# A kernel of attention and two expert layers: one weight loaded by 128 rows, one operand in two transfers, exponentials in another order, and a new order of all steps

## The chip, the cores and the metric

The kernel runs on one core of a Trainium2 chip. The metric is the device time of one launch in microseconds (us), the median of several runs. The core has TensorE (PE, whose weight loads are listed as PEld), VectorE (DVE), ScalarE (ACT), GpSimd (POOL) and SyncE (SP), which issues nearly all transfers here, and 16 DMA engines that carry them out.

## What is computed

Attention over a packed set of 32 rows a head, then a gated layer with a rational function, then one with a cosine. The weights and their inputs `w_in`, `w_out` come as float64.

```python
q, k, v: (8, 8, 576, 64)   p: (8, 8, 32, 64)          # batch, heads, sequence, head size
def sm_attn(qq, kk, vv):
    a = softmax(scale * qq @ kk.T)                    # exp(s - max) / (sum + 1e-9)
    return a @ vv
packed = sm_attn(p, k, v)
x = sm_attn(q, packed, packed)                        # -> x: (4608, 512), heads side by side
h = x @ moe_w_in                                      # 512 x 2048
g = (a0 + a1 h + a2 h^2 + a3 h^3) / (1 + |b0||h| + |b1| h^2 + 1e-6)
y = g @ moe_w_out                                     # 2048 x 512
h = y @ moe2_w_in;  out = (h cos h) @ moe2_w_out
```

## The kernel before

**Stages.** Attention works in 16 units, each of one batch entry and four heads. For a unit, SP loads p, k, q and v (`load`, L461 to L477); PE turns k and q (`trans`, L493) and ACT copies them out of PSUM (`copied`); PE makes the scores of p and k (`scores`, L522), DVE takes their maximum, ACT the exponentials and their sum (`exp1`, L540); PE turns the exponentials in five pieces (`turn_exp`, L558 and L560) and multiplies them with v (`pack`, L573). The packed rows, turned, are kept in DRAM (`keep_pack`, L591) and take part in a second set of scores with q, whose normalized form goes to DRAM as well (`keep_attn`, L631).

**Layer 0** doesn't form x. `m_prod` (L719) multiplies a unit's packed rows with the rows of `w_in` that belong to its heads, and `front` (L769) multiplies the attention weights with the result. 128 steps of ACT, DVE and POOL make the rational function, and `back` (L806) multiplies with `w_out`. Layer 1 loads the result again as x and runs `front` (L785) and `back` for nine blocks of 512 tokens. All large products are made from a high and a low part, so that each is three products.

**The float64 weights.** A tile of 128 x 512 numbers comes as raw words into one of two buffers (`w_load`, L372 for layer 0's w_in, L376 for layer 1's, L381 for w_out). `convert` makes float32 of it in five or six steps: ACT `w_exp` (L389) and `w_low` (L392), DVE `w_abs` (L398) and `w_join` (L408), then for most tiles ACT `w_hi` (L415) and POOL `w_lo` (L420). For layer 0's w_in a tile is made of 64 rows of one head for one block of 512 columns on partitions 0 to 63, and the same rows for the next block on partitions 64 to 127: two transfers of 256 KB. The 16 tiles of w_in and of w_out come in an early and a late half each.

**v.** A unit's v has, in each partition, rows that fit the order in which `exp1` leaves its columns: six transfers, four of 32 partitions with four rows each (L471) and two of 32 partitions with one row (L473).

**The order.** Nothing is scheduled by hand. `Plan.add` records each step with its engine, its costs (busy time, a tail, time on a common DMA bus) and a key, the sum of `FIRST` of its group, `EACH` by its number and `WANTED` of its kind. `Plan.order` then plays the program: of each engine's ready steps it takes, among those that can start within 60 ns, the one with the lowest key. The program is issued in the order of the starts, and every engine keeps to it; waits are semaphores. An SP step counts as 60 ns a transfer (300 for v), whatever is in flight. Group "u" are the first two units, "v" the others, "wi" and "wo" the weights of layer 0, "i" layer 0's steps, "j" layer 1's, "k" the conversion of layer 1's w_in.

Of the kernel before, what the change touches and what calls it, by code (L numbers as in the profile page):

```python
# [9 lines left out]
F32 = mybir.dt.float32  # L10
# [18 lines left out]
class Plan:  # L29
# [11 lines left out]
    WINDOW = 60  # L41

    WANTED = {
        "a2_hi": -80, "a2_lo": 439, "a2_load": -168, "absolute": 238, "back 0": -2,
        "back 0 late": -55, "back 1": 104, "clipped": -277, "copied k": -11, "copied q": -9,
        "cosine": -104, "cubic 0": 1422, "cubic 1": -100, "denom": 166, "done1": -495,
        "done2": -76, "doubled": 32, "exp1": 107, "exp2": 350, "exp_copied": -161, "front 0": -355,
        "front 1": -301, "inverse": 10, "keep_attn": -68, "keep_out": -236, "keep_pack": 207,
        "less_max2": -2, "lin 0": -333, "lin 1": -85, "load k": -12, "load p": -45, "load q": 135,
        "load v": -106, "log": 60, "lower 0": -152, "lower 1": 259, "m_hi": 30, "m_lo": 276,  # L50
        "m_load": 169, "m_prod": -278, "max1": -204, "max2": -287, "open_both": -90,
        "open_left": -65, "open_right": -252, "over 0": 953, "over 1": -66, "pack": 412,
        "packed": -67, "ratio": 60, "recip1": -88, "recip2": -264, "reduced 0": 543,
        "reduced 1": 83, "rounded": -18, "scaled2": -323, "scores 0": -198, "scores 1": -25,
        "slope": -6, "store": 170, "sum2": -36, "taken p": -42, "taken pp": 69, "times": -16,
        "trans k": 107, "trans q": 373, "turn2": 5, "turn_back": -126, "turn_exp": 382,
# [25 lines left out]
    def add(self, eng, busy, key, fn, *args, tail=0, r=(), w=(), new=(), after=(), bus=0, late="", opens=()):  # L82
# [3 lines left out]
        key = self.FIRST[group] + self.EACH[group] * i + off + self.WANTED.get(s.kind, 0)  # L86
        s.eng, s.busy, s.ns, s.key, s.fn, s.args, s.bus = eng, busy, busy + tail, key, fn, args, bus
# [42 lines left out]
    def order(self):  # L130
# [7 lines left out]
        bus = 3000  # L138
# [22 lines left out]
        while len(done) < len(self.steps):  # L161
# [15 lines left out]
            if s.bus:  # L177
# [4 lines left out]
            if s.eng != "-":  # L182
# [33 lines left out]
def pack_attention_moe_moe_kernel(  # L216
# [213 lines left out]
    last_conv = [()]  # L430

    def convert(l, f, which, key, after=()):
        x = (l, f, which)
        group, n, off = key
        bus = 2270 if x[::2] == (1, "i") else 2160 if which == "i" else 1270
        add("SP", 120 if x[::2] == (0, "i") else 60, (group, n, off - 4), w_load, *x, new=[("raw", ("raw", *x), [P, 2 * DM], U32)], bus=bus, after=after)
        add("ACT", 560, key, w_exp, *x, tail=100, r=[("raw", *x)], new=[("sc", ("g", *x), [P, DM], F32)], after=last_conv[0])
        add("ACT", 570, key, w_low, *x, tail=100, r=[("raw", *x)], new=[("sc", ("w", *x), *SC)], after=last_conv[0] if x[::2] == (1, "i") or x == (1, 0, "o") else ())
        s = add("DVE", 603, key, w_abs, *x, tail=85, r=[("g", *x)], w=[("w", *x)])
        if (l, which) == (0, "i"):  # L440
            k2, o = divmod(f, 2)
            home = dict(w=[("win1", k2)]) if o else dict(new=[(f"s{k2}", ("win1", k2), [P, 2 * DM], F32)])
            add("DVE", 604, key, w_join, *x, tail=85, r=[("raw", *x), ("w", *x)], **home)
# [16 lines left out]
    def load(u, nm):  # L460
# [5 lines left out]
        elif nm == "v":  # L466
# [3 lines left out]
            for j in range(4):  # L470
                nc.sync.dma_start(t[32 * j : 32 * (j + 1), :, 0:4, :], rows[:, :, 4 * j : 4 * j + 4, :])  # L471
# [58 lines left out]
    def halves(t):  # L530
        return t[:, :, 0:HS]
# [660 lines left out]
```

## Time and profile before

| | us |
|---|---|
| median of 3 runs (1642.66 to 1646.63) | 1646.03 |
| the profiled execution | 1648.32 |
| its span in the trace | 1646.5 |
| PE busy | 1564.8 |
| DVE busy | 1289.8 |
| ACT busy | 1036.8 |

The profile shows one execution. "Busy" is time in which an engine works; a wait is put down to whom it ended with. DMA shares are the time of packets on the 16 DMA engines, and since packets overlap they can pass 1. The clock is the share of PE's full clock that was granted. Attention takes about the first 200 us, layer 0 goes on beside it and then alone to about 870, layer 1 to the end.

### The profile page before, as it was taken

What the parts mean: (1) busy time and instruction counts of PE and PEld (TensorE: products, weight loads), DVE (VectorE), ACT (ScalarE), POOL (GpSimd) and SP (SyncE); (2) the same over time, 40 slices, a digit from 0 to 9 for tenths busy, and PEclk for the clock granted to TensorE, in tenths of its full rate; (3) what the DMA queues carried; (4) which work ended last, traced back from release to release, by engine and by line L of the source; (5) the groups of instructions that cost most, each with busy time, mean ns of one, the idle gap of its engine ahead of it and who ended that gap; (6) DMA issues with size and microseconds to landing.
All of it is one profiled execution on the core that took longest, in us unless ns stands there. A gap on an engine that the chain in (4) does not pass through costs nothing.

```text
span 1646.5 us, 26978 instructions
## 1 busy us (share of the span) xinstructions
PE 1564.8 (95%) x10176; PEld 1340.0 (81%) x10176; DVE 1289.8 (78%) x2025; ACT 1036.8 (63%) x1745; POOL 343.1 (21%) x274
## 2 busy tenths in 40 slices
PE   4677899999999999999999999999999999999998
PEld 3455688899999989998987878888888888888887
DVE  3588999899999999999899876666666667676664
ACT  4588898999999988998866533333333334343332
POOL 1154334334343343333322200000000000000000
PEclk9899999999999999999999999999999999999999
DMA  9899732212223121215344320201010101001010
GB/s 233 225 273 275 200 92 66 71 48 84 87 66 100 41 88 54 75 41 180 107 152 141 86 65 13 56 17 46 17 39 7 45 1 39 13 22 31 1 26 26
DMA packets 100130, 133.63 MB, mean 81 GB/s; under 512 B 22176, under 2 KB 76960, under 8 KB 100000
## 3 DMA queue, kind: packets, MB, share of 16 engines
q1 hardware_dynamic: 99616, 131.38, 27.8%
q8 instruction: 80, 1.31, 0.3%
q10 hardware_dynamic: 384, 0.52, 0.1%
q14 instruction: 50, 0.41, 0.1%
HBM read 94.11 MB, written 37.75 MB: 80 GB/s over the span
## 4 chain that ended last, share of the span: by engine, by line
PE 77%; ACT 8%; DVE 7%; DMA 5%; issue 2%; SPq 1%; POOL 0%; DVEq 0%; ACTq 0%; POOLq 0%
PE acc L806 41%; PE b L785 23%; PE b L769 9%; DMA raw<-in_moe_w_in_dram 2%; PE b L719 2%; DVE T L893 1%; DMA raw<-in_moe_w_out_dram 1%; ACT T L884 1%; DMA v_in<-in_v_dram 1%; DVE T L895 1%; DVE U L918 1%; PE b L493 1%; DVE T L922 1%; DVE T L918 1%; ACT V L898 1%
## 5 line engine op out<-in xcount | busy, mean ns | idle before, releaser
L806 PE MATMUL acc<-gh,wo 128*128 128x288 f32 x2048 | 417.9, 298 | 2.4 <-ACT gh L950 1.9
L806 PE MATMUL acc<-wo,gh 128*128 128x512 f32 x1152 | 354.9, 389 | 1.4 <-POOL wo L420 1.4
L806 PEld LDWEIGHTS acc<-gh,wo 128*128 128x128 f32 x2048 | 328.2, 188 | 25.5 <-issue 16.6
L806 PE MATMUL acc<-gl,wo 128*128 128x288 f32 x1024 | 301.9, 295 | 2.6 <-DVE gl L953 2.6
L907 POOL TENSOR_TENSOR U<-U,V 128x576 f32<-128x576 f32 x128 | 182.5, 1435 | 369.3 <-DVE T L922 107.7
L806 PEld LDWEIGHTS acc<-wo,gh 128*128 128x128 f32 x1152 | 216.2, 188 | 46.5 <-POOL wo L420 1.7
L886 ACT ACTIVATE T<-b 128x512 f32<-128x512 f32 x144 | 86.0, 597 | 256.6 <-PE b L785 256.2
L806 PE MATMUL acc<-wo,gl 128*128 128x512 f32 x576 | 224.2, 389 | 0.0
L926 DVE TENSOR_SCALAR T<-T 128x512 f32<-128x512 f32 x144 | 62.3, 433 | 189.7 <-ACT T L886 189.0
L806 PEld LDWEIGHTS acc<-gl,wo 128*128 128x128 f32 x1024 | 193.1, 189 | 3.8 <-DVE gl L953 3.8
L950 ACT CAST gh<-V 128x512 fp32r<-128x512 f32 x144 | 89.5, 622 | 111.5 <-PE acc L806 107.4
L941 ACT ACTIVATE U<-U 128x512 f32<-128x512 f32 x144 | 90.6, 629 | 80.3 <-DVE U L937 80.1
L806 PEld LDWEIGHTS acc<-wo,gl 128*128 128x128 f32 x576 | 108.2, 188 | 22.4
L944 DVE TENSOR_TENSOR V<-U,b 128x512 f32<-128x512 f32 x144 | 98.6, 684 | 29.5 <-ACT U L941 25.1
L884 ACT ACTIVATE T<-b,par 128x576 f32<-128x576 f32 x128 | 106.3, 830 | 16.8 <-PE b L769 14.8
L953 DVE TENSOR_TENSOR gl<-T,gh 128x576 fp32r<-128x576 f32 x128 | 108.8, 853 | 9.1 <-PE acc L806 4.5
L901 ACT ACTIVATE U<-V,par 128x576 f32<-128x576 f32 x128 | 111.0, 871 | 0.9 <-DVE T L922 0.2
L953 DVE TENSOR_TENSOR gl<-V,gh 128x512 fp32r<-128x512 f32 x144 | 101.0, 702 | 11.6 <-PE acc L806 11.2
L933 DVE SCALAR_TENSOR_TENSOR U<-T,U 128x512 f32<-128x512 f32 x144 | 105.4, 732 | 3.4
L895 DVE SCALAR_TENSOR_TENSOR T<-T,par,b 128x576 f32<-128x576 f32 x128 | 101.0, 808 | 7.8 <-ACT V L898 6.5
L918 DVE SCALAR_TENSOR_TENSOR U<-U,V 128x576 f32<-128x576 f32 x128 | 100.6, 794 | 7.1 <-ACT V L914 6.6
L893 DVE TENSOR_TENSOR T<-T,b 128x576 f32<-128x576 f32 x128 | 92.9, 745 | 15.8 <-ACT T L884 8.2
(182 smaller groups left out, 3092.8 us busy)
## 6 DMA issues: line engine op xcount, KB each, us to landing
raw<-in_moe_w_out_dram SPq DMA_DIRECT2D x32, 512.0 KB, 3.8
x<-ob SPq DMA_DIRECT2D x24, 576.0 KB, 3.5
k_in<-in_k_dram SPq DMA_DIRECT2D x16, 576.0 KB, 5.7
q_in<-in_q_dram SPq DMA_DIRECT2D x16, 576.0 KB, 7.6
raw<-in_moe_w_in_dram SPq DMA_DIRECT2D x32, 256.0 KB, 5.4
v_in<-in_v_dram SPq DMA_DIRECT2D x64, 128.0 KB, 6.1
raw<-in_moe_w_in_dram SPq DMA_DIRECT2D x16, 512.0 KB, 4.7
w<-sc SPq DMA_DIRECT2D x32, 256.0 KB, 2.2
```

The lines of the kernel that those rows point to most:

```text
L769: nc.tensor.matmul(TILE["h", j][:, e, 0:HS], lhsT=w[:, o : o + P], rhs=x[:, g, :], start=n == 0, stop=n == 3 * NG - 1,)
L785: nc.tensor.matmul(h, lhsT=w[:, ks], rhs=x, start=n == 0, stop=n == 3 * KC - 1)
L806: nc.tensor.matmul(o, lhsT=w, rhs=x, start=i == first and n == 0, stop=i == last and n == len(todo) - 1,)
L884: nc.scalar.activation(T, hidden(j), AF.Identity, scale=par[:, 3:4], bias=par[:, 2:3])
L893: nc.vector.tensor_tensor(T, T, h, op=ALU.mult)
L895: nc.vector.scalar_tensor_tensor(T, T, par[:, 1:2], h, op0=ALU.add, op1=ALU.mult)
L901: nc.scalar.activation(shaped(j, "U"), shaped(j, "V"), AF.Identity, scale=par[:, 5:6], bias=par[:, 4:5])
L907: return nc.gpsimd.tensor_tensor(Q, Q, V, op=ALU.mult)
L918: return nc.vector.scalar_tensor_tensor(t, t, add_, shaped(j, "V"), op0=ALU.add, op1=ALU.mult)
L933: return nc.vector.scalar_tensor_tensor(Y, T, -C2, Y, op0=ALU.mult, op1=ALU.add)
L944: nc.vector.tensor_tensor(shaped(j, "V"), shaped(j, "U"), hidden(j), op=ALU.mult)
L953: return nc.vector.tensor_tensor(shaped(j, "gl"), result(j), shaped(j, "gh").bitcast(F32), op=ALU.subtract)
```

## The change

- **w_in (layer 0):** a tile is now 128 successive rows, those of two heads, for one block of 512 columns, in one transfer of 512 KB onto 128 partitions. Tile t holds heads 2t and 2t+1 for the even block and 2t+1 and 2t+2 for the odd one; where the rows pass 512 (2 of 16 tiles) two transfers remain. `m_prod` finds a head's rows with `rows_at`, so its row halves alternate from product to product, and it reads three tiles where it read two.
- **v:** two transfers a unit: rows 4r to 4r+3 onto partition r for all 128 partitions (512 KB, 1 KB runs), and the last 64 rows onto 64 partitions.
- **Exponentials:** `exp1` writes its results in the order of the keys (a step of 18 elements within a row), so that `turn_exp` reads every fourth element for its four pieces; its last piece is one transpose of 64 columns in place of two products of 32. The pieces of k are no longer turned in a special order.
- **Order:** the planner holds SP to eight transfers in flight and counts 480 ns an issue (`RING`, `ISSUE`), several costs and DMA times are other numbers, the loads of weights are kept in sequence, more kinds of step have a key of their own ("late", "E"), and a table `SHIFT` adds to the key by unit or item. All keys are new.

```diff
+    RING, ISSUE = 8, 480
     WANTED = {
...
     FIRST = {
-        "i": 702.05, "j": 1208.14, "k": 2019.64, "u": -2236.31, "v": -638.77, "wi": -8864.36,
-        "wi late": -3070.04, "wo": -3690.94, "wo late": 1155.49,
+        "i": 220.69, "j": 453.76, "k": 1649.06, "u": -144.84, "v": 113.95, "wi": -3610.16,
+        "wi late": -1623.51, "wo": 597.92, "wo late": -1411.71,
     }
...
+        if group in self.SHIFT:
+            key += self.SHIFT[group][max(0, int(i) // self.PER.get(group, 1))]
...
+            if s.eng == "SP":
+                t = max(t, landed[-self.RING])
...
+            if s.eng == "SP":
+                n, at = s.busy // self.ISSUE, a
+                for _ in range(n):
+                    at = max(at, landed[-self.RING])
+                    bus = max(bus, at + 600) + s.bus / n
+                    landed.append(bus + 1400)
+                    at += self.ISSUE
+                s.end, free["SP"] = bus + 1400, at
...
-            a, h = divmod(f, H)
-            for e in range(2):
-                n = 2 * a + e
-                nc.sync.dma_start(
-                    r64[e * D : (e + 1) * D, :], w_in1[h * D : (h + 1) * D, n * DM : (n + 1) * DM]
-                )
+            t, e = divmod(f, 2)
+            a, t = divmod(t, KC)
+            cols = slice((2 * a + e) * DM, (2 * a + e + 1) * DM)
+            rows = (2 * t + e) * D
+            if rows + P <= DM:
+                nc.sync.dma_start(r64, w_in1[rows : rows + P, cols])
+            else:
+                nc.sync.dma_start(r64[0:D], w_in1[rows : rows + D, cols])
+                nc.sync.dma_start(r64[D:P], w_in1[0:D, cols])
...
-            rows = v[b, hs].rearrange("h (p c) d -> p h c d", c=2 * NT9)
-            for j in range(4):
-                nc.sync.dma_start(t[32 * j : 32 * (j + 1), :, 0:4, :], rows[:, :, 4 * j : 4 * j + 4, :])
-            for e in range(2):
-                nc.sync.dma_start(t[32 * e : 32 * (e + 1), :, 4, :], rows[:, :, 16 + e, :])
+            main = 4 * P
+            nc.sync.dma_start(
+                t[:, :, 0:4, :].rearrange("r h c d -> r h (c d)"),
+                v[b, hs][:, 0:main, :].rearrange("h (r c) d -> r h (c d)", c=4),
+            )
+            nc.sync.dma_start(t[0:D, :, 4, :], v[b, hs][:, main:S, :].rearrange("h r d -> r h d"))
...
-            TILE["e1", u].rearrange("p (a b) -> p a b", a=2),
-            halves(TILE["s", u, 0]),
+            TILE["e1", u].rearrange("r (p t e) -> r e t p", t=NT9, e=2),
+            halves(TILE["s", u, 0]).rearrange("r e (t p) -> r e t p", t=NT9),
...
-        for c in range(4 if a == 0 else 2):
-            first = c % 2 * HS + (c // 2 * P if a == 0 else 2 * P)
-            if a == 0:
-                nc.tensor.transpose(ps[:, c * P : (c + 1) * P], e1[:, first : first + P], ident)
-            else:
-                nc.tensor.matmul(ps[32 * c : 32 * (c + 1), 0:P], lhsT=e1[:, first : first + 32], rhs=ident, start=True, stop=True)
+        if a == 0:
+            for c in range(4):
+                nc.tensor.transpose(ps[:, c * P : (c + 1) * P], e1[:, c : c + 4 * (P - 1) + 1 : 4], ident)
+        else:
+            nc.tensor.transpose(ps[0:D, 0:P], e1[:, 4 * P : S], ident)
...
+    def rows_at(g, h, e):
+        t, half = divmod((g * G4 + h - e) % H, 2)
+        return t, slice(half * D, (half + 1) * D)
...
-                k2, o = divmod(a * H + g * G4 + h, 2)
+                t, rows = rows_at(g, h, e)
...
-                    rhs=TILE["win1", k2][rows, o * DM : (o + 1) * DM],
+                    rhs=TILE["win1", a * KC + t][rows, e * DM : (e + 1) * DM],
```

## Rows read from the trace of the kernel before

**Rows 1.** The page: busy us (share), then tenths of 40 slices of the span.

```profile
PE 1564.8 (95%) x10176; PEld 1340.0 (81%) x10176; DVE 1289.8 (78%) x2025; ACT 1036.8 (63%) x1745; POOL 343.1 (21%) x274
...
DMA  9899732212223121215344320201010101001010
```

**Rows 2.** Engines by stretch: from:to, length, busy PE, PEld, DVE, ACT, POOL, clock, DMA share, GB/s.

```profile
10.00:80.00 70.00, 46.61 (x644) 29.10 (x645) 35.31 (x73) 37.88 (x76) 11.02 (x16) 0.90 0.92 238
80.00:190.00 110.00, 91.57 (x1215) 65.59 (x1212) 94.96 (x175) 93.78 (x180) 54.31 (x50) 0.95 0.92 257
190.00:220.00 30.00, 20.86 (x124) 18.68 (x117) 28.08 (x43) 25.27 (x43) 8.23 (x6) 0.89 0.60 167
220.00:400.00 180.00, 173.57 (x1329) 163.79 (x1329) 164.28 (x223) 164.71 (x272) 68.47 (x49) 0.99 0.20 64
400.00:760.00 360.00, 358.11 (x2818) 339.33 (x2817) 339.54 (x462) 330.98 (x529) 129.12 (x92) 1.00 0.25 80
760.00:880.00 120.00, 112.48 (x740) 103.85 (x739) 107.54 (x156) 94.07 (x155) 40.30 (x30) 1.00 0.42 131
```

**Rows 3.** The chain of waits from 10 to 80 us, shares by line.

```profile
by line: DMA raw<-in_moe_w_in_dram 31.5%; DMA k_in<-in_k_dram 14.8%; PE b L493 13.2%; DMA v_in<-in_v_dram 9.0%; PE b L522 6.8%; PE one L573 5.1%; ACT qT L499 3.0%; ACT kT L499 2.8%; PE b L719 2.8%; ACT sc L392 2.6%; ACT sc L389 2.2%; PE one
```

**Rows 4.** As rows 2, one transfer alone: v; k and q; w_in; layer 1's w_in.

```profile
8.00:10.00 2.00, 0.00 (x0) 0.00 (x0) 1.27 (x2) 0.97 (x3) 0.00 (x0) 1.00 1.07 211
...
16.00:20.00 4.00, 2.71 (x13) 2.07 (x12) 0.00 (x0) 1.37 (x4) 0.00 (x0) 1.00 1.02 417
...
22.00:25.00 3.00, 2.31 (x31) 1.27 (x24) 1.11 (x4) 1.32 (x3) 0.00 (x0) 1.00 1.04 232
...
373.50:374.50 1.00, 1.00 (x10) 1.00 (x9) 0.96 (x2) 0.68 (x1) 1.00 (x2) 1.00 0.98 337
```

**Rows 5.** SP's issues in time: start, us until the last of them, line, count.

```profile
4.17 2.01 SPq L471 DMA_DIRECT2D v_in<-in_v_dram  x4
...
20.46 3.13 SPq L477 DMA_DIRECT2D k_in<-in_k_dram  x2
26.87 0.33 SPq L477 DMA_DIRECT2D q_in<-in_q_dram  x1
```

**Rows 6.** DMA issues: w_in before 10; w_in, v from 10 to 80; v, w_in to 190.

```profile
raw<-in_moe_w_in_dram SPq DMA_DIRECT2D x4, 256.0 KB, 5.4
...
raw<-in_moe_w_in_dram SPq DMA_DIRECT2D x12, 256.0 KB, 9.5
v_in<-in_v_dram SPq DMA_DIRECT2D x18, 128.0 KB, 7.0
...
v_in<-in_v_dram SPq DMA_DIRECT2D x40, 128.0 KB, 6.1
...
raw<-in_moe_w_in_dram SPq DMA_DIRECT2D x8, 256.0 KB, 4.9
```

**Rows 7.** The chain from 186 to 222 us: start, us, what.

```profile
194.68 5.42 DMA raw<-in_moe_w_in_dram
```

**Rows 8.** Durations in ns (least, median, most) by line: strided read, plain cast, exponentials, transposes.

```profile
L389 ACT ACTIVATE sc<-raw x64: 657/672/722, 7.5 to 922.6; 128x512 f32<-128x512 f32 x64
...
L415 ACT CAST wo<-sc x32: 602/620/645, 90.4 to 927.1; 128x512 fp32r<-128x512 f32 x32
...
L540 ACT ACTIVATE e<-b,sm x16: 738/752/791, 23.7 to 175.8; 128x576 f32<-128x576 f32 x16
...
L558 PE MATMUL one<-ident,e x64: 271/273/421, 25.2 to 177.5; 128*128 128x128 f32 x64
```

**Rows 9.** m_prod's products, as rows 8; L806's busy PE and PEld by stretch.

```profile
L719 PE MATMUL b<-s,pt x512: 586/589/1057, 68.2 to 769.7; 64*32 64x512 f32 x171
...
80.00:190.00 110.00, 16.36 (x96) 13.82 (x96) 0.95 0.92 257
```

**Rows 10.** PE in time at the start: start, us, line, [idle before, releaser].

```profile
15.62 0.69 PE L509 MATMUL one<-ident,p_in 128*128 128x128 f32 x2 [15.62 <-POOL p_in L506]
17.60 3.44 PE L493 MATMUL b<-ident,k_in 128*128 128x128 f32 x14 [1.29 <-DMA k_in<-in_k_dram]
```

More of the change, by code (lines that the diff above doesn't have):

```diff
@@ L1 @@
 import math
+from functools import partial
 from contextlib import ExitStack
@@ L49 @@
[L49 to L54, printed above, removed]
@@ new lines @@
+        "load v": -40, "load v late": -161, "log": 130, "log E": 244, "lower 0": -197,
+        "lower 0 E": -245, "lower 1": 42, "m_hi": 793, "m_lo": -878, "m_load": 210, "m_prod": -188,
+        "max1": -207, "max1 late": -84, "max2": -89, "max2 late": -237, "open_both": -151,
+        "open_left": 19, "open_right": 88, "over 0": 25, "over 0 E": -124, "over 1": 23,
+        "over 1 E": 120, "pack": 484, "pack late": 835, "packed": -18, "packed late": 191,
+        "ratio": -8, "ratio E": -597, "recip1": 67, "recip1 late": 532, "recip2": 20,
@@ L434, in convert @@
         group, n, off = key
[L435 to L439, printed above, removed]
+        late = " late" if l == 0 and f >= NF // 2 else ""
+        bus = 1700 if x[::2] == (1, "i") else 1340
+        t = add("SP", 960 if (l, which) == (0, "i") and f % NPR == NPR - 1 else 480, (group, n, off - 4), w_load, *x, late=late, new=[("raw", ("raw", *x), [P, 2 * DM], U32)], bus=bus, after=[*after, *last_load[0]])
+        last_load[0] = (t,)
+        t = add("ACT", 560, key, w_exp, *x, tail=100, late=late, r=[("raw", *x)], new=[("sc", ("g", *x), [P, DM], F32)], after=last_conv[0])
+        add("ACT", 570, key, w_low, *x, tail=100, late=late, r=[("raw", *x)], new=[("sc", ("w", *x), *SC)], after=[t])
+        s = add("DVE", 603, key, w_abs, *x, tail=85, late=late, r=[("g", *x)], w=[("w", *x)])
         if (l, which) == (0, "i"):
@@ L639, in go @@
         def go(eng, busy, fn, *a, off=0, **kw):
-            s = add(eng, busy, key(off), fn, u, *a, **kw)
+            s = add(eng, busy, key(off), fn, u, *a, late="" if u < 2 * NG else " late", **kw)
             names = {o[0] for o in s.objs}
@@ L1023, in operands1 @@
             x = half(c, a * HALF)
-            add("SP", 120, at(j, -60), a2_load, c, x, r=[("a2 out", b * NG + g) for g in range(NG)], new=[("xr", ("a2r", c, x), [P, NG, HS], F32)], bus=880, after=[fronts[j - 7]] if j > 7 else ())
+            add("SP", 960, at(j, -60), a2_load, c, x, r=[("a2 out", b * NG + g) for g in range(NG)], new=[("xr", ("a2r", c, x), [P, NG, HS], F32)], bus=880, after=[fronts[j - 7]] if j > 7 else ())
             add("ACT", 570, at(j, -20), a2_hi, c, x, tail=100, r=[("a2r", c, x)], new=[("a2", ("a2", c, x), [P, 2, NG, HS], F32R)])
@@ L1035, in item1 @@
         key = at(j)
+        add = partial(plan.add, late=" E" if early else "")
         M = [("M", c // 2, i // HALF, g, e) for g in range(NG) for e in "hl"]
@@ L1058, in backs @@
                 home = dict(w=[("acc", 0, c, a, m)]) if i > first else dict(new=[(pool("acc"), ("acc", 0, c, a, m), [P, CH], F32)])
-                s = add("PE", 800, key, back, k, m, tail=170, r=[("gh", k), ("gl", k), ("wo", 0, 2 * i), ("wo", 0, 2 * i + 1)], late=late, **home)
+                s = plan.add("PE", 800, key, back, k, m, tail=170, r=[("gh", k), ("gl", k), ("wo", 0, 2 * i), ("wo", 0, 2 * i + 1)], late=late + " E" * early, **home)
                 if early:
@@ L1097, in item2 @@
         key = at(j)
-        fronts[j] = add("PE", 2775, key, front, j, tail=170, r=[("win2", f), *(("x", c, kk) for kk in range(KC))], new=[("b2", ("h", j), *ps2)], after=[fronts[j - 1]])
+        fronts[j] = add("PE", 2730, key, front, j, tail=170, r=[("win2", f), *(("x", c, kk) for kk in range(KC))], new=[("b2", ("h", j), *ps2)], after=[fronts[j - 1]])
         add("ACT", 520, key, lin, j, tail=100, r=[("h", j)], new=[("T", ("T", j), *W2P)])
@@ L1116, in item2 @@
                     eng = "SP" if queue is nc.sync else "ACT"
-                    add(eng, 450 * len(pieces), key, store, c, m, queue, pieces, r=[("o", c, m)], bus=180 * len(pieces))
+                    add(eng, 480 * len(pieces), key, store, c, m, queue, pieces, r=[("o", c, m)], bus=180 * len(pieces))
     KEEP1, KEEPN = 40, 5.2
```

101 lines of the change are left out of this document (54 added, 47 removed), and 32 rows, old and new, of tables (SHIFT, WANTED).

## The prediction

> **What bounds the kernel now.** I read the page first for where TensorE (PE) is not busy: it works 1564.8 of 1646.5 us, so 81.7 us are idle; the digits of DMA stand at 7 to 9 in the first five slices of 41 us and at 5 or less after them [rows 1]. The table of engines by stretch sizes it [rows 2]: PE, whose first product starts at 15.62 [rows 10], is idle 10.0 us before 10, 23.4 from 10 to 80, 18.4 from 80 to 190, 9.1 from 190 to 220, 6.4 from 220 to 400, 1.9 from 400 to 760 and 7.5 from 760 to 880. From 400 to 760 PE is at 99.5% with VectorE (DVE) at 94.3%: that stretch can give nothing. So what the change is worth is read before 220, from what ends last there. From 10 to 80 the DMA engines are busy 92%, PE 67%, ScalarE (ACT) 54%, DVE 50%: DMA is the bound, and the chain of that stretch says the same, with w_in's loads at 31.5% and v's at 9.0% [rows 3]. From 80 to 190 DMA is again at 92%, but DVE is at 86% and ACT at 85%, so there the next bound is close. I then looked for short stretches in which one kind of transfer runs alone, since a share of 92% does not say whether the bytes move well [rows 4]. They do not: k's and q's packets (128 partitions) move at 417 GB/s, w_in's (64 partitions) at 232, v's (32 partitions) at 211, all with the DMA engines at 1.0 or more of their time. The last view is SP's queue in time [rows 5]: the four issues of a unit's v take 2.01 us, and later two issues of k are spread over 3.13 us from 20.46 and the next one, of q, starts at 26.87: SP waits for landings.
>
> **w_in as 128 rows.** 16 tiles of 512 KB, now two transfers of 256 KB each onto 64 partitions. Now 524,288 B / 232 GB/s = 2.26 us a tile, after at the rate of the 128-partition row 524,288 / 417 = 1.26 us [rows 4]. That is 1.0 us a tile. The bounds are 0 (232 stays) and 1.0 us; I take 1.0, since the row has nearly the same packet (4.6 KB against 4 KB). [...]
>
> **v in two transfers.** The main part is the same 512 KB in the same 1 KB packets, now four transfers onto 32 partitions each, after one onto 128. Now 524,288 / 211 = 2.48 us a unit. The trace has 1 KB packets onto 128 partitions in w_in2's loads: 337 GB/s in the stretch given, so 1.56 us [rows 4]. That is 0.93 us a unit, bounds 0 and 1.2 (at 417). The 64 KB tail keeps its 256 B packets and goes onto 64 partitions: 0.
>
> **Where these lie.** By the counts of issues [rows 6], 4 of w_in's 32 transfers go before 10 us, 12 from 10 to 80, 8 from 80 to 190 and so 8 after; v's 64 go 6, 18 and 40. Up to 80 that is 8 tiles and 6 units: 8 x 1.0 + 6 x 0.93 = 13.6 us, and with every engine at 67% or less I count all of it. From 80 to 190 it is 4 tiles and 10 units, 13.3 us, but DVE's 95.0 us of work in 110 can at best be packed as in the stretch from 400 to 760 (94.3%), into 100.7: 9.3 us are counted. After 190, the chain holds a w_in load of 5.42 us whose conversion stands in DVE's queue ahead of layer 0's steps [rows 7]; two tiles in a row are each 1.0 us shorter: 2.0.
>
> **SP's queue.** v goes from 96 issues to 32, w_in from 32 to 18 (only the tiles whose rows wrap past 512 keep two), 78 fewer at about 0.5 us each [rows 5]. The time is not added: while the DMA engines are at 92% the issues only wait for them. Its use is that larger transfers stand in the queue behind each other, which is the condition of the sum above.
>
> **Exponentials in key order.** exp1 writes with a step of 18 elements (72 B) in place of a contiguous row, and the four transposes of a unit read with a step of 4 elements (16 B). No row shows a strided write of ACT or a strided operand of PE. The nearest row is ACT reading every second word: 672 ns against 620 for the contiguous cast of the same size [rows 8], 0.05 us, so 16 units cost 0.8 us; the other end is the rival below. The transposes stand at 273 ns, 64 of them [rows 8]; I take 0, the other end is doubling, 64 x 0.27 = 17 us of PE. The last piece (two products of 32 columns) becomes one transpose: below 0.3 us a unit either way, 0.
>
> **m_prod.** The eight products of an m_prod keep eight different places (row half and column group), but the halves alternate, and three w_in tiles are needed for two. The first m_prod runs at 68.2 [rows 9], and its third tile belongs to the same early half. I take 0; if the alternating halves made a second pass of 0.59 us, 32 of them cost 19 us where PE is the bound.
>
> **The order.** Every key is new; the planner now charges SP 480 ns for each DMA and holds it to eight in flight, where it charged 60 ns; 480 is what SP's rows show [rows 5]. The loads of w_out lose their place ahead of attention's loads (key about -3640 against about -2250 and -650; now +670 to +1170 against at most about 500), so attention is served first, and k and p ahead of v at the start, where PE now waits 15.62 us for p and then for k behind two units of v [rows 10]. What is late next are the tiles of w_out that layer 0's products (L806) need. No row prices an order. Of the 9.1 us that PE loses from 190 to 220, 2.0 are counted and 1.1 would remain at the rate of 220 to 400 (6.4 / 180 x 30); of the other 6.0 I count half, 3.0, for loads whose landings the order now knows. Bounds: all of 6.0 and the start's 8 us on one side, the 16.4 us of L806 of the rival below on the other.
>
> **Sum.** 13.6 + 9.3 + 2.0 + 3.0 - 0.8 = 27.1 us. The profiled execution took 1648.3 us (span 1646.5, 1.8 around it), 2.3 above the median of 1646.0; the sum takes the one to 1621.2 and the other to 1619.
>
> **Rivals.**
> *PE fills as well* (1590 to 1607, middle 1601): all of 13.6 + 13.3 + 4.0 of DMA time, 8 us of earlier start and 6 us after 190, some 45 us. [...] Against: DVE would have to work at 98% from 80 to 190 (95.0 of 110 - 13.3).
> *The early stretch alone* (1629 to 1641, middle 1635): w_out comes so late that layer 0's products leave the attention stage. They hold 16.4 us of PE from 80 to 190 [rows 9]; if these come after it, 1619 + 16.4. Against: DVE and ACT are relieved of the conversions at the same time.
> *It doesn't do what it says* (1641 to 1651): the rates of 232 and 211 come from the reads and not from the partitions written. Nothing is gained but issues. Against: 1 KB packets reach 337 in [rows 4].
> *The strided exponentials* (1651 and above, about 1653): if each element of exp1 costs four times as much, 0.75 becomes 3.0 us [rows 8], 2.25 us x 10 units on ACT's 93.8 us from 80 to 190: 116.3 us, more than the whole stretch. At 94.3% it takes 123.3 in place of 100.7, 22.6 us, and doubled transposes add 10 x 4 x 0.27 = 11 us of PE: 1619 + 34 = 1653. It decides from about 2.9 us for an exp1. [...]
>
> **How the numbers follow.** A difference under 0.3% (4.9 us) can't be told from none. Forecast (1607 to 1629) 0.50, PE fills too 0.16, early stretch alone 0.14, nothing 0.08, strided exponentials or another loss 0.12. Faster (under 1641): 0.80; within: 0.08; slower: 0.12. The range from 1595 to 1648 leaves out a third of the second case (0.05), a third of the nothing case (0.03) and the last (0.12).
>
> **What would show it.** Right: alone in a stretch, w_in at about 400 GB/s and v at above 330; 18 and 32 issues; attention's last load some 25 us earlier; DVE above 90% from there on. exp1 at 0.8 us and the transposes at 0.27 clear the strided rival, m_prod's products at 0.59 the alternation. Wrong: the same rates; PE at 70% or less between 80 and 160 because it waits for w_out or for a landing; new idle time of PE after 220.

## The result, and the profile after

The changed kernel takes **1624.64 us** (median of 4 runs, 1622.96 to 1628.46) against 1645.08 for the kernel before (median of 4, 1642.66 to 1646.63), measured together: a ratio of 0.988, 95% interval 0.9856 to 0.9904. That is 20.4 us faster. The profiled execution takes 1622.96 us with a span of 1621.1, 25.4 less than the span before; that is more than 20.4 because the profiled execution of before was 3.2 us above its median and this one is 1.7 below.

The page of the changed kernel, busy time and the digits of DMA, to be held against [rows 1]:

```profile
PE 1554.8 (96%) x10128; PEld 1335.6 (82%) x10128; DVE 1293.6 (80%) x2025; ACT 1039.4 (64%) x1745; POOL 344.1 (21%) x274
...
DMA  9995114321221121134554310201010101010010
```

PE's idle time falls from 81.7 to 66.3 us and its busy time by 10.0; together these are the 25.4 us (where the 10.0 come from stands under the prediction's account below). DMA is now at 9 for three slices of 41 us and falls to 1 in the fifth, where it stood at 7 or more for five.

The engines by stretch of the changed kernel (columns as in rows 2):

```profile
10.00:80.00 70.00, 59.35 (x868) 39.67 (x876) 45.28 (x96) 57.49 (x109) 19.28 (x26) 0.90 1.00 329
80.00:190.00 110.00, 93.43 (x1084) 75.19 (x1061) 99.82 (x175) 100.85 (x180) 50.25 (x44) 0.98 0.58 193
190.00:220.00 30.00, 29.75 (x250) 27.37 (x249) 29.32 (x41) 25.82 (x43) 11.76 (x9) 1.00 0.19 65
220.00:400.00 180.00, 167.29 (x1286) 155.14 (x1285) 171.84 (x233) 165.54 (x274) 67.69 (x49) 0.98 0.30 95
400.00:760.00 360.00, 359.15 (x2818) 341.60 (x2818) 345.05 (x463) 328.33 (x529) 131.62 (x93) 1.00 0.24 77
760.00:880.00 120.00, 111.20 (x637) 99.31 (x636) 108.01 (x160) 87.87 (x148) 40.74 (x31) 0.99 0.49 155
```

Against [rows 2], PE's idle time by stretch is:

| stretch, us | before | after |
|---|---|---|
| 10 to 80 | 23.4 | 10.7 |
| 80 to 190 | 18.4 | 16.6 |
| 190 to 220 | 9.1 | 0.25 |
| 220 to 400 | 6.4 | 12.7 |
| 400 to 760 | 1.9 | 0.85 |
| 760 to 880 | 7.5 | 8.8 |

So the early stretch gives 12.7 us, the one from 190 to 220 8.9, and the one from 220 to 400 takes 6.3 back. The granted clock is 0.98 and 1.00 from 80 to 220 where it was 0.95 and 0.89; PE's idle time there is 16.9 us where it was 27.5.

The chain of waits of the changed kernel from 10 to 80 us, shares by line, against [rows 3]:

```profile
by line: PE b L539 23.9%; ACT e L584 9.4%; PE b L566 8.2%; PE one L616 6.8%; PE one L601 5.3%; ACT kT L543 5.3%; issue 5.1%; DMA p_in<-in_p_dram 5.1%; ACT qT L543 4.7%; ACT e1T L608 4.1%; ACT r L656 3.6%; PE one L553 2.5%; PE b L765 1.7%; P
```

w_in's loads, 31.5% of that chain before, are not among its first thirteen lines, nor are v's. PE's turning of k and q (L539) leads, and the exponentials (L584) come second.

Single kinds of transfer in the changed kernel (columns as in rows 2): w_in, k and v:

```profile
16.50:17.40 0.90, 0.00 (x0) 0.00 (x0) 0.45 (x1) 0.90 (x3) 0.00 (x0) 1.00 1.02 405
...
8.50:10.00 1.50, 0.00 (x0) 0.00 (x0) 1.38 (x2) 1.39 (x3) 0.00 (x0) 1.00 1.02 421
...
11.10:11.80 0.70, 0.70 (x5) 0.70 (x4) 0.33 (x1) 0.33 (x1) 0.00 (x0) 1.00 1.11 364
```

w_in moves at 405 GB/s where it moved at 232, v at 364 where it moved at 211 [rows 4]; k is as it was (421 for 417). The sizes of the packets in the trace tell which transfer runs: 4 KB for w_in, 4.6 KB for k and q, 1 KB for v. By them each of these stretches holds one kind alone but for at most 3% of its bytes.

### The profile page after: what moved, and what is told of

Read it like the earlier page. It is cut to its first block, busy times and chain, and to the rows that moved or that the text cites. A ratio compares the mean times of both kernels' runs of the same rounds, so it can differ in the third digit from the quotient of the medians.

```text
span 1621.1 us, 26741 instructions
## 1 busy us (share of the span) xinstructions
PE 1554.8 (96%) x10128; PEld 1335.6 (82%) x10128; DVE 1293.6 (80%) x2025; ACT 1039.4 (64%) x1745; POOL 344.1 (21%) x274
## 4 chain that ended last, share of the span: by engine, by line
PE 76%; ACT 9%; DVE 7%; DMA 3%; issue 2%; POOL 2%; SPq 0%; POOLq 0%; DVEq 0%; ACTq 0%
PE acc L852 39%; PE b L831 24%; PE b L815 8%; PE b L765 2%; PE b L539 1%; DVE gl L999 1%; DVE T L964 1%; POOL U L953 1%; DMA raw<-in_moe_w_in_dram 1%; ACT e L584 1%; ACT T L930 1%; ACT V L956 1%; ACT U L947 1%; ACT V L960 1%; DVE T L939 1%
## 5 line engine op out<-in xcount | busy, mean ns | idle before, releaser
L852 PE MATMUL acc<-gh,wo 128*128 128x288 f32 x2048 | 418.8, 298 | 7.1 <-ACT ob L865 4.1
L852 PE MATMUL acc<-wo,gh 128*128 128x512 f32 x1152 | 354.9, 389 | 0.2
L852 PEld LDWEIGHTS acc<-gh,wo 128*128 128x128 f32 x2048 | 328.5, 188 | 29.8 <-issue 11.8
L852 PE MATMUL acc<-gl,wo 128*128 128x288 f32 x1024 | 302.2, 295 | 2.5 <-DVE gl L999 2.5
L852 PEld LDWEIGHTS acc<-wo,gh 128*128 128x128 f32 x1152 | 216.0, 188 | 45.7 <-DVE xr L873 0.8
L852 PE MATMUL acc<-wo,gl 128*128 128x512 f32 x576 | 224.4, 390 | 0.8 <-DVE gl L999 0.8
L852 PEld LDWEIGHTS acc<-gl,wo 128*128 128x128 f32 x1024 | 193.5, 189 | 3.5 <-DVE gl L999 3.5
L852 PEld LDWEIGHTS acc<-wo,gl 128*128 128x128 f32 x576 | 108.1, 188 | 24.2 <-DVE gl L999 1.7
L990 DVE TENSOR_TENSOR V<-U,b 128x512 f32<-128x512 f32 x144 | 98.5, 684 | 17.3 <-ACT U L987 13.3
L964 DVE SCALAR_TENSOR_TENSOR T<-T,par,V 128x576 f32<-128x576 f32 x128 | 105.1, 823 | 0.1
```

The lines of the kernel that those rows point to most:

```text
L852: nc.tensor.matmul(o, lhsT=w, rhs=x, start=i == first and n == 0, stop=i == last and n == len(todo) - 1,)
L964: return nc.vector.scalar_tensor_tensor(t, t, add_, shaped(j, "V"), op0=ALU.add, op1=ALU.mult)
L990: nc.vector.tensor_tensor(shaped(j, "V"), shaped(j, "U"), hidden(j), op=ALU.mult)
```

## The experiments

Each ratio is to the kernel before, run beside it (its medians were 1645.15, 1645.62 and 1645.8 us in the three groups). A ratio of 0.001 is 1.65 us.

### One part undone, the new order kept

All engines keep the changed kernel's order of steps; only the transfers, or one access pattern, are the old ones.

**x_v6**: v's main part again in four transfers of 32 partitions and its tail in two.

```diff
-            nc.sync.dma_start(
-                t[:, :, 0:4, :].rearrange("r h c d -> r h (c d)"),
-                v[b, hs][:, 0:main, :].rearrange("h (r c) d -> r h (c d)", c=4),
-            )
-            nc.sync.dma_start(t[0:D, :, 4, :], v[b, hs][:, main:S, :].rearrange("h r d -> r h d"))
+            for j in range(4):
+                part, rows = t[32 * j : 32 * (j + 1), :, 0:4, :].rearrange("r h c d -> r h (c d)"), v[b, hs][:, P * j : P * (j + 1), :]
+                nc.sync.dma_start(part, rows.rearrange("h (r c) d -> r h (c d)", c=4))
+            for e in range(2):
+                nc.sync.dma_start(t[32 * e : 32 * (e + 1), :, 4, :], v[b, hs][:, main + 32 * e : main + 32 * (e + 1), :].rearrange("h r d -> r h d"))
```

> The changed kernel, step by step in the same order, but v comes in six transfers again (four of 32 partitions, two for the tail). The theory that the shorter transfers carry the gain: 16 units x 0.9 us are back on the DMA engines, which are busy at 1.00 from 10 to 80 us, so 6 to 14 us are lost of the 20 gained: 1631 to 1639. The rival, that the new order carries it and would hide the longer transfers: under 4 us, 1624 to 1629.

Measured 1644.51 us, ratio 1.0002 (0.9988 to 1.0016): without v's part nothing of the gain is left, some 20 us, more than the 6 to 14 expected.

**x_w2**: every w_in tile in two transfers of 64 partitions.

```diff
-            if rows + P <= DM:
-                nc.sync.dma_start(r64, w_in1[rows : rows + P, cols])
...
+            for x in range(2):
+                at_row = (rows + x * D) % DM
+                nc.sync.dma_start(
+                    r64[x * D : (x + 1) * D], w_in1[at_row : at_row + D, cols]
+                )
```

> The changed kernel in the same order, but each tile of layer 0's w_in comes in two transfers of 64 rows onto 64 partitions. Shorter transfers carry the gain: eight early tiles x 1.0 us are back where DMA is the bound, the late eight lie where it isn't (share 0.2 to 0.3 around 250 us): 5 to 9 us lost, 1630 to 1634. The order carries it: under 3 us, 1624 to 1628.

Measured 1634.59 us, ratio 0.9936 (0.9915 to 0.9957): 9.2 us of the gain go, the upper end of the 5 to 9 expected.

**x_both**: the edits of x_v6 and x_w2 together.

> Both transfers in their old shape, in the new order. Shorter transfers carry the gain: 13 to 22 us lost, 1638 to 1647, that is no better than the kernel before. The order carries it: 1625 to 1632.

Measured 1654.38 us, ratio 1.0057 (1.0037 to 1.0077): the new order with the old transfers is slower than the kernel before, and slower than the 1638 to 1647 expected.

The stretch from 10 to 80 us (columns as in rows 2) in x_v6:

```profile
10.00:80.00 70.00, 52.50 (x678) 33.69 (x681) 36.94 (x80) 49.63 (x94) 11.76 (x18) 0.85 0.95 269
```

In x_w2:

```profile
10.00:80.00 70.00, 54.44 (x751) 36.48 (x752) 42.43 (x91) 55.10 (x105) 15.83 (x22) 0.90 1.02 310
```

And in x_both:

```profile
10.00:80.00 70.00, 52.67 (x662) 32.61 (x662) 35.62 (x77) 48.30 (x92) 10.49 (x17) 0.85 0.99 266
```

The DMA engines are busy in all of them (0.95 to 1.02), as in the changed kernel (1.00), but they move 269, 310 and 266 GB/s against 329: the same work at lower rates. Transfers of w_in alone in x_w2:

```profile
6.00:7.80 1.80, 0.00 (x0) 0.00 (x0) 0.00 (x0) 0.14 (x1) 0.00 (x0) 1.00 1.04 230
```

And transfers of v alone in x_v6 (an eighth of the bytes are its tail's):

```profile
12.50:14.90 2.40, 2.40 (x27) 2.03 (x26) 0.00 (x0) 1.73 (x4) 0.28 (x2) 1.00 1.09 208
```

Onto 64 partitions it is 230 GB/s, onto 32 it is 208: both as in the kernel before (232 and 211 [rows 4]).

**x_expplain**: the first exponential writes a contiguous row (the columns then stand in another order than v's rows, so the packed values differ; the work is the same).

```diff
-            TILE["e1", u].rearrange("r (p t e) -> r e t p", t=NT9, e=2),
-            halves(TILE["s", u, 0]).rearrange("r e (t p) -> r e t p", t=NT9),
+            TILE["e1", u].rearrange("p (a b) -> p a b", a=2),
+            halves(TILE["s", u, 0]),
```

> The changed kernel with exp1 writing its row contiguously as before; the keys are then in the wrong order for the products with v, so the values of the packed rows are not the reference's, and all else is the same. An exp1 takes 1342 ns in the changed kernel against 752; this run should have about 750. If ACT and the chain through exp1 (PE waits 5.9 us for it) end last in the attention stage, 4 to 9 us are gained: 1616 to 1621. If the strided write is hidden behind the transfers: under 2 us.

Measured 1621.28 us, ratio 0.9856 (0.9835 to 0.9877). Beside x_expread below.

### One part done in the kernel before

**b_exp**: the kernel before with its own order; only the exponentials go in key order. What hangs on that order goes with it: the transposes read every fourth element and their last piece is one product, k's pieces are turned in plain order, and v's six transfers bring the rows that fit.

```diff
...
-            TILE["e1", u].rearrange("p (a b) -> p a b", a=2),
-            halves(TILE["s", u, 0]),
+            TILE["e1", u].rearrange("r (p t e) -> r e t p", t=NT9, e=2),
+            halves(TILE["s", u, 0]).rearrange("r e (t p) -> r e t p", t=NT9),
...
```

> The kernel before, in its own order, with the exponentials in key order alone: exp1 writes with a step, the transposes read every fourth element, and v comes in six transfers as before, with the rows that fit. An exp1 should take 1340 ns and not 750, 9.4 us more on ScalarE in all. If the chain through exp1 ends last: 3 to 9 us slower, 1648 to 1655. If the transfers hide it, since DMA is the bound of that stage: under 2 us, 1643 to 1647.

Measured 1645.7 us, ratio 1.0005 (0.9991 to 1.0018): nothing. But not because the instruction is as cheap as I had said. The exponentials in it (columns as in rows 8):

```profile
L544 ACT ACTIVATE e<-b,sm x16: 1338/1344/1386, 22.9 to 173.4; 128x576 f32<-128x576 f32 x16
```

They take 1344 ns against 752 [rows 8]; 16 x 0.59 = 9.5 us of ACT cost no time that can be told here, where the DMA engines are busy 0.96 of the stretch from 10 to 80 us.

**b_v**: b_exp with v in two transfers, as in the change, still in the old order.

```diff
...
-            for j in range(4):
...
-            for e in range(2):
...
+            nc.sync.dma_start(
+                t[:, :, 0:4, :].rearrange("r h c d -> r h (c d)"),
+                v[b, hs][:, 0:main, :].rearrange("h (r c) d -> r h (c d)", c=4),
+            )
+            nc.sync.dma_start(t[0:D, :, 4, :], v[b, hs][:, main:S, :].rearrange("h r d -> r h d"))
...
```

> As the run with the exponentials alone, in the same order, with v in two transfers. If the shape of the transfers is what counts, 16 x 0.9 to 1.0 us leave the DMA engines and 8 to 15 us come off that run: 1635 to 1643. If the gain needs the new order: within 4 us of it.

Measured 1635.76 us, ratio 0.994 (0.9918 to 0.9962): v's part alone is worth 0.0065 over b_exp, 10.7 us. Two stretches of b_exp (columns as in rows 2):

```profile
10.00:80.00 70.00, 47.52 (x667) 30.71 (x675) 37.78 (x78) 45.47 (x86) 12.13 (x17) 0.93 0.96 263
...
190.00:220.00 30.00, 21.04 (x124) 19.33 (x123) 28.17 (x44) 25.28 (x43) 6.80 (x5) 0.89 0.56 155
```

And of b_v:

```profile
10.00:80.00 70.00, 49.05 (x694) 31.57 (x694) 42.47 (x87) 49.74 (x94) 16.12 (x20) 0.95 1.04 314
...
190.00:220.00 30.00, 27.00 (x170) 25.72 (x169) 28.21 (x42) 28.36 (x48) 8.51 (x6) 0.85 0.41 118
```

The DMA engines move 314 GB/s for 263. PE's idle time falls by 1.5 us from 10 to 80 and by 6.0 from 190 to 220.

**b_all**: b_v with w_in as 128 rows, under the old planner and its keys. m_prod then needs three tiles, so the planner plays the program anew and the order is not that of before.

```diff
...
-            for e in range(2):
...
+            if rows + P <= DM:
+                nc.sync.dma_start(r64, w_in1[rows : rows + P, cols])
...
-                k2, o = divmod(a * H + g * G4 + h, 2)
+                t, rows = rows_at(g, h, e)
...
```

> All new paths (w_in by 128 rows, v in two transfers, exponentials in key order) with the keys, costs and rules of the planner before, so that only the order is not the new one; m_prod waits for three tiles, so the planner moves it behind the eighth early tile. If the new order adds nothing of its own: within 5 us of the changed kernel, 1620 to 1630. If the order is worth as much as the transfers: 1635 to 1645.

Measured 1689.24 us, ratio 1.0268 (1.0242 to 1.0293): slower, and outside both ranges expected. The loss stands at the changeover to layer 1, in three stretches of 60 us (columns as in rows 2):

```profile
820.00:880.00 60.00, 46.41 (x237) 38.82 (x236) 46.64 (x68) 31.77 (x54) 16.35 (x12) 0.91 0.36 123
880.00:940.00 60.00, 51.48 (x195) 40.61 (x195) 36.18 (x60) 27.89 (x47) 12.67 (x10) 0.89 0.31 94
940.00:1000.00 60.00, 49.36 (x187) 38.49 (x186) 40.37 (x66) 27.98 (x48) 11.53 (x9) 0.89 0.25 76
```

PE's longest wait in b_all from 820 to 1000 us (who waits for whom: us in total, times, longest):

```profile
PE b L789 <- DVE V L948: 25.8, 11, 3.8
```

PE works 147.3 of these 180 us, at a clock of 0.89 to 0.91; the kernel before works 175.4, at 1.00, and waits 2.2 us for that step. Layer 1's products wait for the cosine steps of DVE. Which of the replanned steps puts these late isn't shown by this run, and so it doesn't price w_in's rows; it says that the old keys can't carry them. Nor is a gain of theirs seen ahead of that loss: up to 820 us PE is idle 68.9 us in b_all, 68.1 in b_v and 55.0 in the changed kernel.

### Where the strided side of the exponential lies

**x_expread**: the changed kernel and its order, but ACT walks the scores in key order, so that it reads PSUM with a step and writes one run.

```diff
-            TILE["e1", u].rearrange("r (p t e) -> r e t p", t=NT9, e=2),
-            halves(TILE["s", u, 0]).rearrange("r e (t p) -> r e t p", t=NT9),
+            TILE["e1", u].rearrange("r (p t e) -> r p t e", t=NT9, e=2),
+            halves(TILE["s", u, 0]).rearrange("r e (t p) -> r p t e", t=NT9),
```

> The changed kernel in the same order, with exp1 going through its elements in the order of the keys: it reads PSUM with steps and writes a contiguous row, with the reference's result. If only the strided write costs: an exp1 near 750 ns and the time of the run with plain exponentials, 0.985 to 0.987 of before. If the strided read costs as much: 1340 ns or more and 0.988 to 0.990.

Measured 1622.19 us, ratio 0.9852 (0.9822 to 0.9882). The exponentials of the changed kernel (columns as in rows 8):

```profile
L584 ACT ACTIVATE e<-b,sm x16: 1327/1342/1382, 16.2 to 126.0; 128x576 f32<-128x576 f32 x16
```

And those of x_expread:

```profile
L584 ACT ACTIVATE e<-b,sm x16: 720/742/766, 16.1 to 123.0; 128x576 f32<-128x576 f32 x16
```

The same numbers reach the same places, 742 ns against 1342: the step in the write costs 0.6 us, the step in the read nothing (the plain row took 752 [rows 8], and 744 in x_expplain).

### The last group: partitions or number of transfers

**a_again** is the changed kernel as it is, and **x_expread_b** is x_expread once more, beside it.

> The changed kernel as it is, beside the others of this call. 1622 to 1628 us, 1.1 to 1.4% under the kernel before. It is the partner for the runs of this call.

> The first exponential walks the scores in key order and writes one run, a second time, now beside the changed kernel on the same chip. If the strided write costs the path what the last runs suggest (4 to 5 us of the 9.4 us that sixteen exponentials of 0.59 us more take), it is 2 to 6 us under the changed kernel, 1617 to 1622 us. If ACT had the room, as the prediction took it, the two are within 1 us.

Measured 1628.08 us, ratio 0.989 (0.987 to 0.9911), and 1622.2 us, ratio 0.9857 (0.9837 to 0.9876). The intervals overlap by a little; but the three runs without the strided write stand at 0.9852, 0.9856 and 0.9857 and the changed kernel at 0.988 and 0.989. I read a gain of 2 to 6 us of the 9.6 us of ACT time, and a version faster than both kernels; its size is no better known than that. The spans of the profiled executions differ less (1619.6 and 1618.7 against 1621.1 and 1620.2), so the place of the gain isn't settled. What the trace does show is the chain of x_expread_b from 10 to 80 us:

```profile
by line: PE b L539 21.6%; PE b L566 9.9%; PE one L616 7.6%; DVE r L643 5.3%; issue 4.6%; ACT e1T L608 4.5%; ACT kT L543 4.2%; PE one L601 3.8%; ACT qT L543 3.7%; DVE sm L578 3.1%; DVE mx L648 3.1%; ACT r L656 2.7%; DVE sc L447 2.3%; ACT e L
```

The exponentials, 9.4% of that chain in the changed kernel, stand behind the entry of 2.3% here.

**x_vheads**: the changed kernel with a unit's v in six transfers again, but the main part's four are one head each onto all 128 partitions (the tail's two are two heads each, onto 64).

```diff
-            nc.sync.dma_start(
...
-            nc.sync.dma_start(t[0:D, :, 4, :], v[b, hs][:, main:S, :].rearrange("h r d -> r h d"))
+            for h in range(G4):
+                rows = v[b, hs][h, 0:main, :].rearrange("(r c) d -> r (c d)", c=4)
+                nc.sync.dma_start(t[:, h, 0:4, :].rearrange("r c d -> r (c d)"), rows)
+            for h in (0, 2):
+                nc.sync.dma_start(t[0:D, h : h + 2, 4, :], v[b, hs][h : h + 2, main:S, :].rearrange("h r d -> r h d"))
```

> The changed kernel's order; v's unit again in six transfers, but each onto all 128 partitions (four of one head's main keys, two of the tail's). Theory A, it is the partitions that a transfer reaches that set its rate: within 3 to 5 us of the changed kernel, 1623 to 1630 us. Theory B, it is the number of transfers (SP's issues and the queue's slots): most of the 20 us that six transfers onto 32 partitions cost comes back, 1640 to 1645 us.

Measured 1638.79 us, ratio 0.9958 (0.9942 to 0.9974). Between the two theories: of the 18.4 us between x_v6 (1.0002) and a_again (0.989), 7.2 come back with the full partitions and 11.2 stay with the number. The trace of x_vheads shows how: first 10 to 80 us, then v alone, then two stretches in which the engines aren't full (columns as in rows 2).

```profile
10.00:80.00 70.00, 55.37 (x743) 37.34 (x743) 42.17 (x88) 52.87 (x100) 14.82 (x22) 0.90 0.89 287
...
11.20:11.80 0.60, 0.60 (x5) 0.58 (x3) 0.08 (x1) 0.44 (x1) 0.09 (x1) 1.00 1.11 355
11.90:13.10 1.20, 1.20 (x7) 0.99 (x6) 0.00 (x0) 0.74 (x2) 0.25 (x2) 1.00 0.56 157
14.30:16.60 2.30, 1.87 (x34) 0.52 (x33) 0.78 (x2) 0.81 (x3) 0.00 (x0) 1.00 0.62 155
```

And SP's issues in it (columns as in rows 5):

```profile
12.12 2.02 SPq L522 DMA_DIRECT2D v_in<-in_v_dram  x4
14.18 1.26 SPq L524 DMA_DIRECT2D v_in<-in_v_dram  x2
15.56 0.98 SPq L420 DMA_DIRECT2D raw<-in_moe_w_in_dram  x2
```

Here the DMA engines are no longer full (0.89): v alone moves at 355 GB/s, but SP needs 2.02 us for the four of a unit, 0.5 us each, which is 131,072 B / 0.5 us = 262 GB/s and less than the engines can move. They run dry (0.62 from 14.3 to 16.6) until SP gets to the next large transfer at 15.56. In x_v6 it was the other way round: full engines that moved 269 GB/s.

The number of transfers costs in a second way too. SP's waits in x_vheads from 8 to 14 us (who waits for whom: us in total, times, longest):

```profile
SPq L524 <- DMA k_in<-in_k_dram: 1.9, 2, 1.1
SPq L522 <- DMA raw<-in_moe_w_in_dram: 1.0, 1, 1.0
```

SP waits with v's issues (L522, L524) for landings of k and w_in, which v doesn't need. The traces of both kernels have at most eight transfers in flight (first at 5.75 us before, at 6.13 after), though the planner of before knows no such limit; what sets it isn't shown. When k has landed, what stands in the queue are small pieces of p and v, and the engines fall to 0.56 from 11.9 to 13.1 us. How the 11.2 us divide between the issues and these waits isn't shown.

**x_wcols**: the changed kernel with the 14 tiles of w_in that lie together in two transfers of 256 columns, each onto 128 partitions.

```diff
-                nc.sync.dma_start(r64, w_in1[rows : rows + P, cols])
+                [nc.sync.dma_start(r64[:, x : x + 256], w_in1[rows : rows + P, cols.start + x : cols.start + x + 256]) for x in (0, 256)]
```

> The changed kernel's order; each w_in tile of 128 rows that lie together comes in two transfers again, each of half the columns onto all 128 partitions. Theory A, partitions: 1624 to 1628 us, within 3 us of the changed kernel. Theory B, number of transfers: as with two transfers of 64 partitions, about 1634 us.

Measured 1624.95 us, ratio 0.9881 (0.9861 to 0.9901): as the changed kernel, 9 us under x_w2, with the same number of transfers as that. Two stretches of x_wcols, transfers of w_in alone, and 10 to 80 us:

```profile
6.50:7.20 0.70, 0.00 (x0) 0.00 (x0) 0.00 (x0) 0.01 (x1) 0.00 (x0) 1.00 1.06 407
...
10.00:80.00 70.00, 57.65 (x848) 38.49 (x854) 44.67 (x95) 56.95 (x109) 18.65 (x26) 0.93 1.01 327
```

For w_in it is the partitions alone: these transfers read runs of 2 KB, shorter than the 4 KB of x_w2, and are faster all the same (407 GB/s against 230). Two transfers of 256 KB are large enough: at 407 GB/s one takes 0.64 us, longer than an issue of 0.5; one of 128 KB of v takes 0.37 at 355 and is shorter.

## Why the prediction was right, and where its steps were not

The sign, the time (1619 against 1624.64, the profiled execution 1621.2 against 1622.96) and the bound were right. The sum was 27.1 us where 20.4 came: w_in's, v's and the order's terms were each too large, by 3.6, 1.4 and 2.3 us as measured below. By the intervals of the runs each of these differences is known to some 4 or 5 us, so the parts are less firm than the total. By steps:

**What bounds the kernel: shown.** With the old transfers and nothing else changed, the whole gain goes (x_v6, x_both), and the stretch from 10 to 80 us shows full DMA engines that move less. The rival by which the rates come from the reads is refuted for w_in by x_wcols; for v the packets stay at 1 KB throughout, but which rows one transfer reads changes along with its partitions (x_vheads), so there it is argued.

**w_in, 12.8 us in the sum (8.0, then 4.0 of 13.3 of the 9.3 counted, 2.8, then 2.0): 9.2 measured** (x_w2; 7.6 against a_again). The rate came as the row of 128 partitions had it, 405 GB/s for 417, and a transfer of fewer partitions loses it (230 in x_w2 against 407 in x_wcols). The term of 8 tiles before 80 us, 8.0, by itself comes near what was measured. The 2.8 and 2.0 for the other eight tiles have no place left: the new order moves most of these out of the stage that waits for DMA. The changed kernel's issues of w_in from 0 to 80, and from 190 to 300 us (count, KB each, median us to landing):

```profile
raw<-in_moe_w_in_dram SPq DMA_DIRECT2D x7, 512.0 KB, 6.4
raw<-in_moe_w_in_dram SPq DMA_DIRECT2D x2, 256.0 KB, 7.0
...
raw<-in_moe_w_in_dram SPq DMA_DIRECT2D x5, 512.0 KB, 3.9
raw<-in_moe_w_in_dram SPq DMA_DIRECT2D x2, 256.0 KB, 4.1
```

Eight tiles (one of them in two transfers) lie before 80 us, as before, but six after 190, where the DMA share is 0.19 and 0.30 and a shorter transfer has nothing to relieve; two are left in between, where I had counted four. That the other eight gave nothing is argued from this; no run undoes them alone. I had left their places as they were though I had said that the order is new.

With packets of 4 KB the rate is 230 to 232 GB/s onto 64 partitions and 405 onto 128, with packets of 1 KB 208 to 211 onto 32 and 337 to 364 onto 128. What makes a transfer onto fewer partitions slower no trace shows.

**v, 12.1 us in the sum (5.6 and 9.3 of 13.3 of the 9.3 counted, 6.5): 10.7 in the old order** (b_v against b_exp), so its size holds. Its place isn't shown: of b_v's gain in PE's idle time 1.5 us lie from 10 to 80 and 6.0 from 190 to 220, where the sum had 5.6 before 80 and 6.5 from 80 to 190. In the new order it carries 18 to 20 us (x_v6), and there the full partitions alone are worth 7.2 (x_vheads), though their rate was all that the term priced.

**SP's queue, "the time is not added": wrong in the new order.** I took the issues to wait for the engines in any case. x_vheads shows 11.2 us that hang on the number of v's transfers alone: pieces of 128 KB go faster than SP issues them once they reach all partitions (0.37 against 0.5 us), and SP waits for landings between them (2.9 us from 8 to 14 us). For w_in's pieces of 256 KB it holds (x_wcols).

**The exponentials, 0.8 us: wrong in size.** One costs 0.59 us more, not 0.05: the row of every second word read was the wrong neighbour for a write with a step of 72 B. With the old transfers this is covered (b_exp, 1.0005), and that b_exp's 0.8 us look like the 0.8 of the sum is luck: the price was too low by a factor of more than ten, and the time was hidden. With the new transfers it costs 2 to 6 us. The rival with four times the price, an assumption that no row shows, was too high: 1342 ns against 742 without the step in the write is 1.8 times, and below the 2.9 us from which it would decide.

**The transposes and m_prod: near enough nothing.** The transposes' weight loads in the kernel before, then three lines of the changed kernel, the transposes' weight loads and products and m_prod's products (columns as in rows 8):

```profile
L558 PEld LDWEIGHTS one<-ident,e x64: 138/141/231, 25.1 to 177.4; 128*128 128x128 f32 x64
...
L601 PEld LDWEIGHTS one<-ident,e x64: 195/212/231, 17.6 to 129.1; 128*128 128x128 f32 x64
L601 PE MATMUL one<-ident,e x64: 273/285/490, 17.6 to 129.3; 128*128 128x128 f32 x64
...
L765 PE MATMUL b<-s,pt x512: 589/589/1040, 51.9 to 739.0; 64*32 64x512 f32 x171
```

The products stay at 273 at least and 285 in the middle (273 [rows 8]), m_prod's at 589 [rows 9]; the alternating halves cost nothing. The weight loads are 0.07 us longer, 4.5 us in all; loads and products overlap (PEld is busy 1335.6 us and PE 1554.8 of a span of 1621.1).

**The order, 3.0 us: not shown.** With w_in by 64 partitions and the exponentials in key order there are all four cases (w_in's tiles hold other rows in the new order, and m_prod needs three of them there): old v in the old order 1.0005 and in the new 1.0057; new v in the old order 0.994 and in the new 0.9936. The new order gains nothing that can be told with the new v (0.7 us), and loses 8.6 with the old one. The old keys can't carry w_in's rows (b_all), so what these would be worth in an old order stays open, and their 9.2 us come with the new one. The steps from before to after, measured, are 10.7 (v) + 0.7 (order) + 9.2 (w_in) - 0.8 (b_exp) = 19.8, against 20.4 for the whole; since each run is held against the one before it in this row, the sum must come out, and it is no proof of the parts. By the other way round, transfers last, the order costs 8.6 us (x_both against b_exp) and the transfers give 29.

One reading of the order was wrong. I took the loads of w_out to lose their place; the first is issued at 48.2 us in the changed kernel and at 78.4 before. So the rival in which w_out comes too late doesn't happen: `back` of layer 0 has more of PE from 80 to 190 us, not less (L852 there, 30.1 us for 16.4; columns as in [rows 9]):

```profile
80.00:190.00 110.00, 30.09 (x197) 26.95 (x198) 0.98 0.58 193
```

**PE's own time: no term in the sum.** Of the 25.4 us between the two spans 10.0 are PE's busy time. The pages of b_exp and of x_both, which have the 10128 products of the changed kernel:

```profile
PE 1561.9 (95%) x10128; PEld 1341.3 (82%) x10128; DVE 1289.9 (78%) x2025; ACT 1044.2 (64%) x1745; POOL 342.4 (21%) x274
...
PE 1566.8 (95%) x10128; PEld 1343.7 (81%) x10128; DVE 1298.5 (79%) x2025; ACT 1040.2 (63%) x1745; POOL 344.1 (21%) x274
```

The same products take PE 1566.8 us at a mean granted clock of 0.982 (x_both), 1561.9 at 0.988 (b_exp) and 1554.8 at 0.991 (the changed kernel), where 1 is the full clock. So where PE waits less, its own work is shorter as well: of the 10.0 us, 2.9 are there in b_exp already, with 48 fewer products than before, and 7.1 come between b_exp and the changed kernel. The clock's 0.3% of 1562 would be some 5 of these, an estimate; the rest is open.

**What bounds after it: DVE and ACT, as said; a part is given back, as not said.** From 80 to 190 us both now do more than before (99.8 and 100.9 us for 95.0 and 93.8), and the last exponential starts at 126.0 us in place of 175.8 [rows 8]; k's, q's and v's loads end 28 us earlier (the last lands at 148.9 in place of 177.4), where I had said some 25. But PE gains only 1.8 us there. It works 82% of the time from 80 to 160, so the sign of 70% or less did not come. From 220 to 400 DVE is at 95% (171.8 of 180) where it was at 91%, and PE's longest waits in that stretch of the changed kernel (columns as for b_all) are these, of which the first came to 5.1 us in the kernel before:

```profile
PE b L815 <- DVE T L941: 7.8, 4, 5.5
PE acc L852 <- ACT ob L865: 3.0, 4, 1.6
```

That is the "new idle time of PE after 220" which the prediction named as a sign against it, 6.3 us. The rival in which PE fills as well is refuted by the time and by this.

**The earlier start isn't shown to give anything by itself.** PE's first product starts at 10.1 us in place of 15.6, but at 11.2 in x_both, which is slower than before. The changed kernel's longest waits of PE from 10 to 190 us (same columns) show what follows the start:

```profile
PE b L539 <- DMA k_in<-in_k_dram: 10.1, 1, 10.1
PE b L539 <- ACT e L584: 5.9, 8, 2.0
PE b L539 <- ACT qT L543: 3.1, 6, 0.8
```

After the one wait for the first k, it waits for ACT, not for a landing; the second line is the exponential.

## What to carry to other kernels

A DMA share of 90% or more says that the engines are occupied, not that they move much (0.92 went with 238 GB/s before, 1.00 with 329 after): look for stretches with one kind of transfer alone, which the packets' sizes tell, and compare their GB/s by the number of partitions they reach. Give each transfer all 128 (405 GB/s against 232 onto 64 for w_in here) and so many bytes that it lasts longer than SP's issue of the next, some 0.5 us here. Where a permutation must go into an instruction of ACT, put the step on the side that reads PSUM (742 ns here, 1342 with the step in the write) and measure the write before pricing it. And a cost that is hidden under one bound has to be priced again for the bound that comes after it.

## What the runs showed that I had not expected

- ACT writing 576 words with a step of 72 B takes 1342 ns where a run takes 742; reading PSUM with the step takes 742 as well.
- PE's weight load with a step of 16 B takes 212 ns in the middle against 141 in the kernel before. PE's loads and products overlap (1335.6 and 1554.8 us busy of 1621.1). b_exp has it too and is no slower than before; with the new transfers no run prices it.
- 256 KB onto 128 partitions move at 407 GB/s, onto 64 at 230 to 232; 128 KB onto 32 move at 208, and onto 128 at 355, where SP is the one that can't keep up.
- The traces of both kernels have at most eight transfers in flight, and in x_vheads SP waits 2.9 us, from 8 to 14 us, for landings that its next transfers don't need.
- Two orders of the same steps can differ in sign with the transfers under them: the new one costs 8.6 us more than the old with v in six transfers and is level with it with two.
